# One DMA queue in another order, a table of priorities tuned again, a head by token halves, and a last tile in two half-banks, in a list-scheduled attention and GEGLU kernel

## The chip, the cores and the metric

The kernel runs on one core of one Trainium2 chip. The metric is the device time of a whole execution in microseconds (us). The kernel before takes 278.9 us as the median of three runs (278.46 to 281.0). The record marks all runs below as fast, but for the single runs (unknown) and one of the kernel before at 281.44 us (slow). A profile of a run covers the span from the first instruction to the last landing; that is 1.7 to 1.8 us less than the time of the same run.

## The reference, cut to what matters

`x` is 2048 tokens of 512 features in bf16. Path A is attention in four segments of 512 tokens with 32 heads of 16, plus a memory that is carried from segment to segment. Path B is a GEGLU of width 1792. A sigmoid gate mixes both.

```python
for s in range(4):
    logits = einsum('bhqd,bhkd->bhqk', qs, ks) * scale + mask
    a_dot  = einsum('bhqk,bhkd->bhqd', softmax(logits), vs)
    a_mem  = phi(qs) @ M / (phi(qs) @ z + 1e-6)          # memory of the segments before
    outs.append(g * a_mem + (1 - g) * a_dot)
    M = M + phi(ks)^T @ vs ; z = z + sum(phi(ks))        # phi(t) = t+1 if t > 0 else exp(t)
a = concat(outs) @ wo
b = (gelu(x @ w_gate) * (x @ w_up)) @ w_down
out = gate * a + (1 - gate) * b
```

## The kernel before

The program is a list of tasks. A list scheduler, which runs when the kernel is built, gives each task an engine and a place, using estimates of durations, priorities (`BIAS`, by kind of task) and a small model of the DMA queue. What it emits is one instruction stream per engine, with semaphore waits. All transfers go through one queue, SP's, in program order. So the order of that queue follows from the model:

```python
            cur[e] = t.finish
            avail = t.finish
            if t.nbytes:                                   # a transfer: 0.5 us (transpose 1.25) on SP, then it is on its way
                dma_free = max(t.finish + 2.2, dma_free) + t.nbytes / DMA_RATE
                avail = dma_free
```

The model lets SP issue a transfer every 0.5 or 1.25 us however much is on its way. The parts that the change touches are these (`# ...` marks cuts):

```python
    # loads, in order of rank: x0, wk, wq, wv, small vectors, wg, then
    xdma(1)                                                # x block 1, four DMA transposes
    wdma(("wu", 0), SP, ...); wdma(("wu", 1), SP, ...)
    wdma("wd", SP, ...); wdma("wo", SP, ...)
    for i in range(9):                                     # warm-up matmuls on zeros
        # ...
    for kb in range(4):                                    # x0 transposed on TensorE, 4 per feature block
        task(f"x0t{kb}", PE, [... e.transpose(XB[...], xin[:, a, ...], ident) for a in range(4)])
        # one eviction of 128x512 per block, on ACT or DVE
    # memory(s): phi(k), transposed through memory, then the outer products with v
            for t in range(4):
                dma(f"pkT{s}_{t}", SP, lambda t=t: phkt[:, :, t * 128:(t + 1) * 128], lambda t=t: kT[:, t, :],
                    [("kT", t)], [("phkt", t)], 131072, issue=1.25, transpose=True)
    # downs(s): the last tile of the last segment accumulates in one bank, one scale, one store
    # order of the tasks in the list:
    prep(0); memory(0); attention(0); xdma(2); prep(1); gates_copied(0); gates_copied(1)
    # ...
```

The softmax here doesn't subtract the row's maximum and nothing guards it: scores larger than these inputs give would overflow.

Of the kernel before, what the change touches and what calls it, by code (L numbers as in the profile page):

```python
# [13 lines left out]
ALU = mybir.AluOpType  # L14
# [13 lines left out]
DMA_RATE = 330.0e3  # L28
PATIENCE = 3.0
# [4 lines left out]
    "D0": -167, "D1": -801, "D2": 83, "D3": -2, "G0": -198, "G1": -253, "G3": -13, "GdT1": -249, "GdT2": 532,  # L34
    "GdT3": 9, "Gev1": -32, "K0": 433, "K1": 30, "K2": 94, "K3": -21, "Q0": -84, "Q1": -59, "Q2": 313, "Q3":
    -15, "U0": -1382, "U1": -543, "U2": -1, "U3": -8, "Um0": 173, "Um1": 323, "Um2": 15, "Um3": 17, "V0": 59,
    "V3": -41, "Vev0": 134, "Vev3": 374, "Vlo0": -111, "Vlo1": -31, "Vlo3": -24, "den1": 619, "den2": 394,
    "den3": 85, "denp1": 4, "denp2": 30, "denp3": 155, "exp0": -59, "exp1": -37, "exp3": 73, "exsT0": 537,
    "exsT2": 14, "exsT3": 341, "fin1": 62, "fin2": 650, "fin3": 478, "gate0": 8, "gate1": 52, "gate2": 216,
    "gate3": -16, "gelu0": -177, "gelu1": 530, "gelu2": 12, "gelu3": 107, "gexs0": 15, "gexs1": -66, "gexs2":  # L40
    278, "gexs3": 91, "gts0": -2, "gts1": -12, "gts2": -10, "gts3": -2, "kl0": 15, "kl1": 571, "kl2": 26,
    "kl3": 15, "kp0": 23, "kp1": 107, "kp2": -4, "msk0": 84, "msk1": -40, "msk2": 160, "msk3": 113, "mz0":
    402, "mz1": -18, "mz2": 72, "mzacc0": -37, "mzacc1": -9, "mzacc2": -32, "mzbd0": -100, "mzbd1": 12,
    "mzbd2": 43, "norm0": 124, "norm1": -731, "norm2": 11, "norm3": 226, "num1": 30, "num2": 47, "num3": -3,
    "nump1": 419, "nump2": -30, "oTd1": -2, "oTd2": 163, "oTd3": -179, "omg": 518, "pkT0": 8, "pkT1": 25,
    "pkT2": -8, "pkc0": -408, "pkc1": 4, "pkc2": -57, "pke0": 30, "pke1": -29, "pke2": -52, "pqc1": 40,
    "pqc2": 36, "pqe1": 118, "pqe2": 4, "pqe3": -13, "pv0": 271, "pv1": -58, "pv2": -63, "pv3": 146, "pvt0":
    -321, "pvt1": -8, "qk0": 61, "qk1": 34, "qk2": -377, "qk3": 96, "x1": -417, "x2": 6, "x3": -10
# [69 lines left out]
class Sched:  # L118
# [32 lines left out]
    def schedule(self):  # L151
# [35 lines left out]
        while len(order) < n:  # L187
# [31 lines left out]
            t.finish = st + t.est[e]  # L219
            if e == PE:  # L220
                if t.tiled == "pv" and last_pe == "pv":
                    t.finish -= PV_JOIN
                last_pe = t.tiled
            cur[e] = t.finish
            avail = t.finish
            if t.nbytes:
                dma_free = max(t.finish + 2.2, dma_free) + t.nbytes / DMA_RATE
                avail = dma_free
# [132 lines left out]
def _build(es, nc, A_x, A_wq, A_wk, A_wv, A_wo, A_beta, B_w_gate, B_w_up, B_w_down, gate_w, out):  # L361
# [94 lines left out]
    def dma(name, eng, out_ap, in_ap, reads, writes, nbytes, issue=0.5, transpose=False, bias=0.0, sm=None,  # L456
            nonc=False):
        sm = sm if sm is not None else sem("d")

        def f(e):  # L460
            if transpose:
                return e.dma_start_transpose(out_ap(), in_ap())  # L462
            if nonc:
                with nc.allow_non_contiguous_dma(reason="small vector"):
                    return e.dma_start(out_ap(), in_ap())
            return e.dma_start(out_ap(), in_ap())
        return task(name, eng, [Instr(f, reads, writes, issue, dma_sem=sm)], bias=bias, nbytes=nbytes)
# [3 lines left out]
    def wdma(key, eng, dst, src, nbytes, nonc=False):  # L471
        rank[0] -= 20.0
        dma("w_" + str(key), eng, lambda: dst, lambda: src, [], [("w", key)], nbytes, bias=rank[0], nonc=nonc)

    def xdma(s):
        for kb in range(4):
            rank[0] -= 20.0
            dma(f"x{s}_{kb}", SP, lambda kb=kb: xT[s % NX][:, kb, :],
                lambda kb=kb: A_x[0, s * 512:(s + 1) * 512, kb * 128:(kb + 1) * 128],
                [], [("xT", s % NX, kb)], 131072, issue=1.25, transpose=True, bias=rank[0] if s < 2 else 0.0)  # L480
# [30 lines left out]
    wdma(("wu", 0), SP, wu[:, :, 0:half], wur[:, :, 0:half], 917504)  # L511
    wdma(("wu", 1), SP, wu[:, :, half:DF], wur[:, :, half:DF], 917504)
    wdma("wd", SP, wd[:], r4(B_w_down), 1835008)
    wdma("wo", SP, wo[:], r4(A_wo), 524288)

    for i in range(9):
        gw = Grp(banks)
        task(f"warm{i}", PE, [Instr(lambda e, gw=gw: e.matmul(gw.f32()[:, :], warm[:, 0:128], warm, start=True,  # L518
                                                              stop=True), [wkey], [gw.key], 0.43)],
             grp=gw, bias=5000.0 - i)  # L520
    XB = XALL.bitcast(BF)
    for kb in range(4):
        task(f"x0t{kb}", PE, [Instr(lambda e, kb=kb, a=a: e.transpose(  # L523
            XB[:, kb * 1024 + a * 128:kb * 1024 + (a + 1) * 128], xin[:, a, kb * 128:(kb + 1) * 128], ident[:, :]),
            [("hT", 1, a), ("c", "ident")], [("X", kb)], mm_t(128)) for a in range(4)])
        src = XB[:, kb * 1024:kb * 1024 + 512]
        S.add(Task(f"x0ev{kb}", {
            ACT: [Instr(lambda e, kb=kb, src=src: e.activation(xT[0][:, kb, :], src, ACTF.Copy), [("X", kb)],
                        [("xT", 0, kb)], act_t(512))],
            DVE: [Instr(lambda e, kb=kb, src=src: e.tensor_copy(xT[0][:, kb, :], src), [("X", kb)],  # L530
                        [("xT", 0, kb)], dve_t(512, 2))]}))
# [56 lines left out]
    def proj_T(name, s, t, w, wkey, dst, wkeys, even=None):  # L588

        g = Grp(banks)  # L590
        xs = xT[s % NX]
        pieces(name, g, [mm(g, lambda: g.f32()[:, :], w[:, kb, t * 128:(t + 1) * 128], xs[:, kb, :],
                            [("xT", s % NX, kb), ("w", (wkey, t > 0))], kb == 0, kb == 3, 512)
                         for kb in range(4)], 2)
        if even is not None:
            task(name + "even", ACT, [Instr(lambda e: e.activation(even[0], g.f32()[:, :], ACTF.Copy,
                                                                   scale=maskc[0][:, 0:1]),
                                            [g.key, ("c", "mask", 0)], [even[1]], act_t(512, ap=True))], grp=g)
        copy_out(name + "ev", g, lambda: dst[:, t, :], lambda: g.f32()[:, :], [g.key], wkeys, 512)
# [32 lines left out]
    def prep(s):  # L632
# [21 lines left out]
        for tile in range(4):  # L654
            g = Grp(banks)
            pieces(f"V{s}_{tile}", g, [mm(g, lambda g=g: g.f32()[:, :], xT[x3][:, kb, tile * 128:(tile + 1) * 128],
                                          wv[:, kb, :], [("xT", x3, kb), ("w", "wv")], kb == 0, kb == 3, 512)
                                       for kb in range(4)], 2)
            copy_out(f"Vev{s}_{tile}", g, lambda tile=tile: Vaug[sl][:, tile, :, :, 0:16],
                     lambda g=g: g.f32()[:, :].rearrange("p (i j e) -> p j i e", j=2, e=16), [g.key],  # L660
                     [("Vaug", sl, tile)], 512)
        for j in range(2):
# [5 lines left out]
                                   [("xT", x3, kb), ("w", "gatew")], kb == 0, kb == 3, 1)  # L668
# [22 lines left out]
        if s > 0:  # L691
# [14 lines left out]
            for qt in range(4):  # L706
# [13 lines left out]
                    lambda qt=qt: otok[:, qt % 2, :], [("otok", qt % 2)], [("oT", sl, qt, t) for t in range(4)], 131072,  # L720
                    issue=1.25, transpose=True)

    def memory(s):
        sl = s % 2
        if s < NSEG - 1:
            for i in range(2):
                phi_task("pk", s, s, kT, "kT", kT, "kT", i)
            for t in range(4):
                dma(f"pkT{s}_{t}", SP, lambda t=t: phkt[:, :, t * 128:(t + 1) * 128], lambda t=t: kT[:, t, :],
                    [("kT", t)], [("phkt", t)], 131072, issue=1.25, transpose=True)  # L730
# [132 lines left out]
    def gate_mms(s, ft):  # L863
# [3 lines left out]
                                    [("xT", x3, kb), ("w", ("wg", ft // 7))], kb == 0, kb == 3, 512)  # L867
# [43 lines left out]
    def ups(s):  # L911
        sl, x3 = s % 2, s % NX
        for ft in range(NFT):
            g = Grp(banks)
            pieces(f"U{s}_{ft}", g, [mm(g, lambda g=g: g.f32()[:, :], wu[:, kb, ft * 128:(ft + 1) * 128],
                                        xT[x3][:, kb, :], [("xT", x3, kb), ("w", ("wu", ft // 7))], kb == 0,
# [5 lines left out]
    def downs(s):  # L922
# [3 lines left out]
        for tile in range(4):  # L926
            gt = 4 * s + tile
            on_x = last and tile == 3
            g = None if on_x else Grp(banks)
            key = ("X", 0) if on_x else g.key  # L930
            view = (lambda: X[0]) if on_x else (lambda g=g: g.f32()[:, :])
# [3 lines left out]
                   for fb in range(NFT)]  # L935
            seq = dwn + att if last else att + dwn
            ins = [mm(g, view, a, b, rd, i == 0, i == len(seq) - 1, 512, fkey=key)
                   for i, (a, b, rd) in enumerate(seq)]
            dep = hdep + (fins if last else [S._w[("oT", sl, tile, 3)]])
# [4 lines left out]
                    ostage[tile % N_OST][:], view(), ACTF.Copy, scale=omgt[:, gt:gt + 1]), rd, [("ost", tile % N_OST)],  # L944
                    act_t(512, ap=True))],
                DVE: [Instr(lambda e, view=view, gt=gt, tile=tile: e.tensor_scalar(  # L946
                    ostage[tile % N_OST][:], view(), omgt[:, gt:gt + 1], None, ALU.mult), rd, [("ost", tile % N_OST)],
                    dve_t(512, ap=True))]}, grp=g))
# [7 lines left out]
    sem_out = [sem("so") for _ in range(16)]  # L956
    gate_head()
# [3 lines left out]
    xdma(2)  # L961
# [29 lines left out]
    with nc.Block() as block:  # L991
# [17 lines left out]
        def _(e):  # L1009
            em.emit_stream(SP)  # L1010
            for sm in sem_out:
# [47 lines left out]
```

## Time and profile before

| | before |
|---|---|
| time, median of 3 | 278.9 us |
| span of the profiled run (its time) | 276.2 us (277.97) |
| TensorE (PE) busy | 262.9 us, 95% |
| ScalarE (ACT), VectorE (DVE), GpSimd (POOL) busy | 76%, 68%, 35% |
| PE waits for DMA, 30 to 41 us | 2.6 us |

PE is the bound. Its weight loads have a row of their own, PEld. A page of this profile is read from the top: the span, then the busy time of each engine, then the slices of a fortieth of the span each, where a low digit in PE's row is a place to look at. The waits say who ended the idle time; the timeline of SP's queue says when a transfer was issued. The lines themselves stand in the prediction. One caution, which the prediction missed: the page counts 2913 PE instructions against 2954 weight loads, so 41 matmul records are missing from this trace.

### The profile page before, as it was taken

Reading aid. Unit: us, or ns where it says so; the run is one execution under the profiler, and the core shown is the slowest. Engines: PE = TensorE matmul, PEld = TensorE weight load, DVE = VectorE, ACT = ScalarE, POOL = GpSimd, SP = SyncE. Lnnn points to the kernel's source line nnn. Section 1 sums busy time; section 2 is a strip of 40 time slices with the busy share of each in tenths; the row PEclk is TensorE's granted clock in tenths of the full one; section 3 lists DMA queues with packets and bytes.
Section 4 is the critical chain, followed back from the end, with each engine's and each line's share of the span. In section 5 each row is a group of like instructions: output and inputs, shape, how many; then the busy total and the mean of one; then the engine's idle time right before and its main releaser. Section 6 shows DMA issues by size and latency. Waiting matters only on the chain.

```text
span 276.2 us, 6911 instructions
## 1 busy us (share of the span) xinstructions
PE 262.9 (95%) x2913; PEld 121.2 (44%) x2954; DVE 187.6 (68%) x330; ACT 211.1 (76%) x178; POOL 97.5 (35%) x223
## 2 busy tenths in 40 slices
PE   8999869999999999999999999999999999989995
PEld 4444334534544444544344444444354444434442
DVE  1778738877797897797552896698752534797451
ACT  3789838999899797788978989887868777757602
POOL 8377613442101743353300762443300253352300
PEclk9999999999999999999999999999999999999999
DMA  6999960100310141123020110000020022000002
GB/s 166 290 300 357 216 125 2 23 18 2 41 40 2 38 78 38 40 42 58 20 43 0 40 33 28 21 23 19 2 44 0 19 62 56 23 0 2 0 2 76
DMA packets 31879, 16.51 MB, mean 60 GB/s; under 512 B 21352, under 2 KB 31848, under 8 KB 31848
## 3 DMA queue, kind: packets, MB, share of 16 engines
q1 hardware_dynamic: 31848, 16.07, 24.8%
q8 instruction: 23, 0.38, 0.6%
q14 instruction: 8, 0.07, 0.1%
HBM read 8.14 MB, written 2.10 MB: 37 GB/s over the span
## 4 chain that ended last, share of the span: by engine, by line
PE 85%; ACT 6%; DVE 4%; issue 2%; SPq 1%; DMA 1%; ACTq 0%; DVEq 0%
PE psW L435 68%; PE psXALL L763 8%; PE psW L812 4%; PE psW L518 1%; PE psXALL L435 1%; ACT pt L770 1%; ACT hT L897 1%; SPq L462 1%; PE psW L820 1%; ACT L897 1%; DMA phkt<-kT 1%; ACT ptl L770 1%; ACT hT L886 1%; PE psXALL L523 1%; DVE kT L610 1%
## 5 line engine op out<-in xcount | busy, mean ns | idle before, releaser
L770 ACT ACTIVATE pt<-psXALL 128x2048 bf16<-128x2048 f32 x64 | 120.0, 1875 | 31.6 <-PE psXALL L763 24.0
L774 POOL TENSOR_SCALAR_AFFINE_SELECT pt<-pt 128x256 bf16<-128x256 bf16 x128 | 57.1, 446 | 146.8 <-ACT pt L770 108.5
L435 PE MATMUL psW<-xT,wu 128*128 128x512 bf16 x215 | 51.1, 379 | 2.2 <-DVE hT L918 1.2
L435 PE MATMUL psW<-xT,wg 128*128 128x512 bf16 x218 | 50.2, 379 | 0.8 <-issue 0.5
L435 PE MATMUL psW<-wd,hT 128*128 128x512 bf16 x197 | 49.0, 379 | 1.4 <-issue 1.1
L918 DVE TENSOR_TENSOR hT<-psW,hT 128x512 bf16<-128x512 f32 x56 | 37.5, 686 | 13.7 <-PE psW L435 12.9
L827 DVE STREAM_TRANSPOSE tb<-psW 128x512 f32<-128x512 f32 x32 | 21.2, 697 | 22.9 <-PE psW L820 22.9
L435 PEld LDWEIGHTS psW<-xT,wg 128*128 128x128 bf16 x224 | 21.0, 98 | 25.3 <-issue 1.5
L435 PEld LDWEIGHTS psW<-xT,wu 128*128 128x128 bf16 x224 | 20.4, 98 | 25.9 <-DVE hT L918 1.9
L435 PEld LDWEIGHTS psW<-wd,hT 128*128 128x128 bf16 x210 | 19.0, 98 | 22.5 <-issue 2.3
L897 ACT ACTIVATE hT<-psW 128x512 bf16<-128x512 f32 x28 | 16.2, 598 | 7.0 <-PE psW L435 6.9
L774 POOL TENSOR_SCALAR_AFFINE_SELECT ptl<-ptl 128x2048 bf16<-128x2048 bf16 x8 | 17.1, 2141 | 8.7 <-ACT ptl L770 8.5
L812 PE MATMUL psW<-pt,vaug 128*17 128x192 bf16 (+3 forms) x512 | 18.8, 273 | 0.2 <-ACT hT L897 0.2
L770 ACT ACTIVATE ptl<-psXALL 128x2048 bf16<-128x2048 f32 x8 | 15.0, 1877 | 4.7 <-PE psXALL L763 4.6
L682 POOL COPY exsT<-exs 32x4 f32<-32x4 f32 x64 | 14.5, 227 | 7.6 <-ACT exs L671 3.9
L452 DVE CAST hT<-psW 128x512 bf16<-128x512 f32 x20 | 13.7, 687 | 4.8 <-PE psW L435 4.6
L435 PE MATMUL psW<-xT,wq 128*128 128x512 bf16 x59 | 15.8, 380 | 1.1 <-DMA xT<-in_A_x_dram 0.6
L435 PE MATMUL psW<-xT,wk 128*128 128x512 bf16 x63 | 15.5, 380 | 0.1
L435 PE MATMUL psW<-wo,oT 128*128 128x512 bf16 x56 | 15.1, 380 | 0.5 <-issue 0.3
L435 PE MATMUL psW<-wv,xT 128*128 128x512 bf16 x61 | 14.0, 379 | 0.4 <-ACT hT L886 0.2
L946 DVE TENSOR_SCALAR ost<-psW,omgt 128x512 bf16<-128x512 f32 x9 | 6.6, 746 | 10.8 <-PE psW L435 9.3
L812 PEld LDWEIGHTS psW<-pt,vaug 128*17 128x17 bf16 x512 | 10.3, 90 | 8.3 <-issue 3.4
(99 smaller groups left out, 305.8 us busy)
## 6 DMA issues: line engine op xcount, KB each, us to landing
out_dram<-ost SPq DMA_DIRECT2D x16, 128.0 KB, 1.7
wg<-in_B_w_gate_dram SPq DMA_DIRECT2D x2, 896.0 KB, 7.3
wd<-in_B_w_down_dram SPq DMA_DIRECT2D x1, 1792.0 KB, 11.0
wu<-in_B_w_up_dram SPq DMA_DIRECT2D x2, 896.0 KB, 11.0
vlow<-vaug SPq DMA_DIRECT2D x8, 136.0 KB, 2.8
hT<-in_A_x_dram SPq DMA_DIRECT2D x2, 256.0 KB, 2.9
wv<-in_A_wv_dram SPq DMA_DIRECT2D x1, 512.0 KB, 6.3
wo<-in_A_wo_dram SPq DMA_DIRECT2D x1, 512.0 KB, 12.0
```

The costliest lines, as they stand in the source:

```text
L435: return Instr(lambda e: e.matmul(view(), lhsT, rhs, start=first, stop=last), reads=reads, writes=[fkey if fkey is not None else g.key], e ...
L452: alts[DVE] = [Instr(lambda e: e.tensor_copy(dst(), src()), reads=reads, writes=writes, est=dve_t(n))]
L462: return e.dma_start_transpose(out_ap(), in_ap())
L682: cross = task(f"exsT{s}", POOL, [Instr(lambda e, g=g, c=c: e.tensor_copy(exsT[sl][32 * g:32 * g + 32, c:16:4], exs[32 * c:32 * c + 32, s4 ...
L763: instrs.append(Instr(lambda e, g=g, lhs=lhs, rhs=rhs, c0=c0, ncol=ncol: e.matmul(X[g][:, c0:c0 + ncol], lhs(32 * g), rhs(32 * g), start=T ...
L770: prev_exp[0] = exp_task(s, f"exp{s}_{t}{name}", [Instr(lambda e: e.activation(dst[:], XALL[:, :].rearrange("p (g c) -> p g c", g=4), ACTF ...
L774: task(f"msk{s}_{t}{name}", POOL, [Instr(lambda e, view=view, pat=pat, base=base: e.affine_select(out=view, in_=view, compare_op=ALU.is_ge ...
L812: instrs.append(Instr(lambda e, t=t, q=q, kb=kb, slot=slot, c0=c0: e.matmul(gp.f32()[32 * q:32 * q + 17, 128 * kb + 64:512], Vaug[sl][:, k ...
L827: task(f"pvt{s}_{t}_{j}", DVE, [Instr(lambda e: e.transpose(Tb[:, j, :], gp.f32()[:, :]), [gp.key], [("Tb", j)], dve_t(512))], grp=gp)
L897: lambda e, g=g, ft=ft, s=s: e.activation(hT[s % 2][:, ft, :], g.f32()[:, :], ACTF.Gelu_apprx_tanh),
L918: task(f"Um{s}_{ft}", DVE, [Instr(lambda e, g=g, ft=ft: e.tensor_tensor(hT[sl][:, ft, :], g.f32()[:, :], hT[sl][:, ft, :], ALU.mult), [g.k ...
L946: DVE: [Instr(lambda e, view=view, gt=gt, tile=tile: e.tensor_scalar(ostage[tile % N_OST][:], view(), omgt[:, gt:gt + 1], None, ALU.mult), ...
```

## The change

The intent: the transposes of phi(k) of segment 0 should not queue behind 4.2 MB of weights and a third x block (0.5 MB) that are needed later; the first projection should start as soon as the first half of x0 is there; the last output should leave sooner. The model of the queue is mended too (a transfer holds SP up once 3 us of data is waiting, transposes count double), and the table of priorities is tuned again.

```diff
+DMA_LAT = 1.6
+DMA_BACKLOG = 3.0
 BIAS = { ... }                      # all values new (cut)
+            if t.nbytes:
+                t.finish = max(t.finish, dma_free - DMA_BACKLOG)
-                dma_free = max(t.finish + 2.2, dma_free) + t.nbytes / DMA_RATE
+                dma_free = max(t.finish + DMA_LAT, dma_free) + t.nbytes / DMA_RATE
-                [], [("xT", s % NX, kb)], 131072, issue=1.25, transpose=True, ...
+                [], xk(s, kb), 262144, issue=1.25, transpose=True, ...          # also pkT, oTd: 262144
-    for i in range(9):
+    for i in range(6):
-    for kb in range(4):
-        task(f"x0t{kb}", PE, [... for a in range(4)])            # one eviction of 512
+    for u in range(2):
+        for kb in range(4):
+            gx = Grp(banks) if u else None                        # second half through the psW banks
+            task(f"x0t{kb}_{u}", PE, [... for a in range(2)], grp=gx)  # one eviction of 256
     ...
+            if on_x:                                              # the last tile: two banks of 256 columns
+                for part in (dwn, att):
+                    for u in range(2): ...                        # 14 + 14, then 4 + 4 matmuls of 256
+                # half 0 scaled on ACT, half 1 on DVE, one store of 64 KB each
     attention(0)
-    xdma(2)
+    pk0 = [t for t in S.tasks if t.name == "pkT0_3"]
+    xdma(2, after=pk0)
+    wdma(("wu", 0), SP, ..., after=pk0); wdma(("wu", 1), SP, ..., after=pk0)
+    wdma("wd", SP, ..., after=pk0); wdma("wo", SP, ..., after=pk0)
     prep(1)
```

## The prediction

> **What bounds the kernel now.** I read four views of the kernel before, in this order: the page's busy table and slices, the busy time of the engines by stretches, the waits of the tensor engine, and the timelines around the places where it stood still. The first two lines to read are the span and the tensor engine's busy time.
>
> ```profile
> span 276.2 us, 6911 instructions
> PE 262.9 (95%) x2913; PEld 121.2 (44%) x2954; DVE 187.6 (68%) x330; ACT 211.1 (76%) x178; POOL 97.5 (35%) x223
> PE   8999869999999999999999999999999999989995
> ```
>
> PE works in 262.9 of 276.2 us; ACT, the next, has 76%. So only 13.3 us of the span can be won by filling gaps, plus whatever PE work is taken out. The PE row of the slices has low digits in the first slice, around the sixth (35 to 41 us), near the end (245 us) and in the last. The stretches give their sizes (columns: stretch, its length, then busy us of each engine, clock, DMA share, GB/s).
>
> ```profile
> 1.26:30.00 28.74, 28.43 (x211) 12.94 (x214) 18.23 (x45) 21.52 (x30) 20.22 (x56) 1.00 1.01 299
> 30.00:40.00 10.00, 7.16 (x61) 2.98 (x64) 5.44 (x11) 5.68 (x6) 3.14 (x7) 1.00 1.18 145
> 40.00:245.00 205.00, 200.76 (x2380) 93.58 (x2408) 147.05 (x249) 170.11 (x135) 67.10 (x143) 1.00 0.14 29
> 245.00:250.00 5.00, 3.69 (x29) 1.42 (x25) 4.92 (x6) 2.73 (x2) 2.49 (x3) 1.00 0.00 0
> 250.00:273.20 23.20, 22.88 (x246) 10.24 (x246) 11.71 (x20) 9.90 (x7) 4.14 (x10) 1.00 0.06 18
> ```
>
> PE idle is 1.26 us before its first matmul, 0.31 to 30 us, 2.84 between 30 and 40, 4.24 over the next 205 us, 1.31 at 245, 0.32 after it, and 3.0 of output after its last matmul. The 4.24 are pieces of 0.05 and 0.16 us, mostly behind the small attention-times-value matmuls; I take them as fixed. What made the 2.84 us is in the waits of 30 to 41 us and in the timeline.
>
> ```profile
> ACT pt L770 <- PE psW L812: 3.6, 1, 3.6
> PE psW L435 <- DMA phkt<-kT: 2.0, 3, 0.9
> PE psW L435 <- DMA xT<-in_A_x_dram: 0.6, 1, 0.6
> ```
>
> PE waited three times, 2.0 us, for transposes of phi(k) of segment 0 through memory (phkt), and 0.6 us for a projection of the third x block. ACT lost 3.6 us to the same hold-up: its next exponential could not start. The issuing queue's own timeline says why those transposes came so late.
>
> ```profile
> 15.32 3.71 SPq L466 DMA_DIRECT2D wo<-in_A_wo_dram  x1
> 19.07 3.74 SPq L466 DMA_DIRECT2D wu<-in_B_w_up_dram  x2
> 22.86 9.08 SPq L462 DMA_TRANSPOSE xT<-in_A_x_dram  x4
> 32.07 0.71 SPq L466 DMA_DIRECT2D vlow<-vaug  x1
> 32.82 1.79 SPq L462 DMA_TRANSPOSE phkt<-kT  x1
> 34.66 0.59 SPq L466 DMA_DIRECT2D vlow<-vaug  x1
> 35.30 3.93 SPq L462 DMA_TRANSPOSE phkt<-kT  x3
> ```
>
> One queue issues everything in program order. The second half of phi(k) was written on DVE by 22.0 us (the add that starts at 21.34 takes 0.69), yet its transposes were issued from 32.8 to 39.2: the queue was first occupied with wo, wu and the third x block for 16.5 us. The two small copies of v (vlow) that the first attention-times-value matmuls need sat behind them too.
>
> **What the Trainium skill says.** First, "DMA: Bandwidth & Descriptors", section "Anatomy of one DMA": a semaphore wait of a DMA happens on the issuing sequencer, before dispatch. Hence an early entry blocks all later ones, and the order in the queue is a real lever; the lines above agree. Second, the same page, "Issuing engines are not separate DMA queues": all share 16 engines, so moving loads moves their traffic rather than shrinking it; 10 to 35 us runs at 294 GB/s here. Third, "TensorE: Matmul & The Clock Gate", Part 1: a cold array passes half its pulses, so a 512-column matmul costs 426.7 ns cold and 215.7 warm, and the switch comes with a free-running activity window of about 3.4 us. The trace agrees: nine warm-up matmuls take from 1.26 to 5.07 us plus a tail, weight loads start 0.427 us apart, and from 6.74 us on ten matmuls in a row take 2.33 us, or (2.33 - 0.38)/9 = 0.217 each. Fourth, its Part 4 says that transposes in the array do not count as activity in the same way; no view here shows that, but it makes cutting warm-up work a risk.
>
> **The change part by part.**
>
> (1) Six warm-up matmuls for nine: it takes out 3 x 0.427 = 1.28 us of filler. It pays only as far as x0 is there. Its two loads were issued at 0.81 and about 1.3 us and took 2.8 and 3.1 us to land, so the halves are there at about 3.6 and 4.4; the warm-up would end at 1.26 + 6 x 0.427 = 3.8. Before, the 16 transposes ran from 5.07, 0.107 us apart, and the first projection began at 6.74. Now by halves: eight transposes from about 3.9 to 4.75, eight more to 5.6, then one short eviction. ACT took 0.60 and DVE 0.43 us for 512 columns; 256 columns should be about 0.39 and 0.29. The first projection starts at about 6.0, 0.7 earlier. But the clock was seen fast only from about 6.7, so matmuls in that 0.7 us run at half speed and about 0.35 is given back; and some 0.2 more where PE waits anyway at 10.7 us for wq, whose load is not moved. I count **-0.3**, with plus or minus 1 for the clock's window.
>
> (2) The queue's order: wu, wd, wo and the third x block go behind the fourth transpose of phi(k). Those can then be issued from about 17.5 (first half of phi(k) done) to 24 us, and vlow once the last v eviction at about 18 us is done. Landing at 2.5 to 5 us, they are there by 28, before the sixth exponential. So the waits for phkt (2.0 us) go, the 0.6 us wait for the third x block goes because the retuned order need not take that projection so early, and the rest of the 2.84 shrinks with them. The moved loads cost nothing: wu is first read at 78.6 us and wd at 102.8; with 4.6 MB at the 294 GB/s seen, 16 us of traffic from about 25 us ends near 45. ACT regains its 3.6 us, so it does not become the new limit. I count **-2.6**.
>
> (3) The last output tile in half-banks: 36 matmuls of 256 columns for 18 of 512. At half of 0.217 plus about 2.5 ns fixed each, 36 x 0.111 = 4.0 against 18 x 0.217 = 3.9: +0.1. What follows the last matmul is then a 256-column DVE scale instead of an ACT one of 0.69 us. DVE took 0.75 for 512 columns, so about 0.45 for 256; the other half overlaps on ACT with PE's last matmuls. The out transfer of half the size keeps its fixed part (1.7 us to landing for 128 KB). -0.25 and +0.1 give **-0.15**.
>
> (4) The retuned priorities and transfer estimates reorder the whole list. They can remove the 1.15 us wait for a DVE multiply at 245 us (half of its 1.31 us stretch counted: -0.65), or bring one like it elsewhere. I count **-0.5**.
>
> Sum: -0.3 - 2.6 - 0.15 - 0.5 = -3.55, on 278.9: about 275.3 us. The weight of PE's real matmuls stays.
>
> **The rivals.** (a) *A new wait takes the old one's place*: phi(k) is transposed early but while wg and the first x block's successors still load (wg's second half is issued at 14.1), so transposes issue at the 2 us apiece of the x transposes rather than 1.25, and land late; or the moved loads now hold up the transposes of attention output. For it: the DMA share of 1.25 at 10 to 15 us. Against: wg's 0.9 MB is through by about 21 us, and before, phkt came even later. It would halve part 2: 276.7. (b) *The clock stays cold one window longer* because six warm-ups and transposes do not fill it: up to 3.4 us at half speed, +1.7, giving 277. For it: the skill's sentence on transposes; against: projections follow immediately. The three timed runs differ by 2.5 us (278.46 to 281.0), which could be this. (c) *Everything fits*: all 1.28 us of part 1, all 2.84 of part 2, all 1.31 at 245 us and 0.25 at the end, sum 5.7 or 273.2 us. That is just past 2%, and hard to exceed since PE remains the bound. (d) *The gap was hidden anyway*: against it stands that PE itself is the idle engine there, and the chain of waits runs through that very transfer (2.47 us of phkt).
>
> **Range and chances.** The centre is 275.3. The low end, 272.7, is rival (c) with half a microsecond of small gaps gone too; the high end, 278.2, is (a) and (b) together. A gain of over 2% means under 273.3, nearly the whole of (c): 0.12. Slower by over 2% means 284.5, which no part explains: 0.02. The rest, 0.86, is within 2%.
>
> **What would show it.** Right: phkt transposes issued before 25 us with no DMA wait of PE between 25 and 45; ACT's 3.6 us pause gone; PE busy down by about 1.3 us, its idle between first and last matmul about 6 instead of 9; first projection near 6 us; tail after the last matmul near 2.75 us. Wrong: new PE waits over 0.5 us on DVE or DMA in the reordered list, matmuls still cold past 8 us, or an ACT stall that moves to another segment.

## The result, and the profile after

The changed kernel takes 271.99 us (median of 4 runs, 271.44 to 272.78) against 279.28 for the kernel before (4 runs). The ratio is 0.9733 with a 95% interval of 0.968 to 0.9787. A ratio here is the mean time of one kernel's fast runs over that of the other's in the same rounds, so it isn't quite the ratio of the medians. The prediction was 275.3 with 272.7 as the low end, so the gain of 7.3 us was twice what was expected, and the time lies 0.7 us below the range.

The page of the changed kernel, first lines and PE's slices:

```profile
span 270.3 us, 6945 instructions
...
PE 260.6 (96%) x2928; PEld 122.1 (45%) x2969; DVE 186.9 (69%) x333; ACT 211.4 (78%) x180; POOL 96.5 (36%) x223
...
PE   7999999999999999999999999999999999999996
```

The row of nines has no dip left between the first slice and the last. The stretch of 30 to 40 us (stretch, length, busy us of PE, PEld, DVE, ACT, POOL, clock, DMA share, GB/s):

```profile
30.00:40.00 10.00, 9.79 (x129) 4.32 (x130) 8.22 (x18) 8.74 (x8) 7.62 (x27) 1.00 1.35 289
```

And all that PE waited for a transfer, from the view of waits (who waits, for whom: us in all, times, the longest):

```profile
PE psW L439 <- DMA wk<-in_A_wk_dram: 0.4, 1, 0.4
```

PE is busy for 9.79 us there instead of 7.16, and ACT for 8.74 instead of 5.68. Its only wait for a transfer is 0.4 us for wk in the head. SP's queue shows why (start, us of issue, what):

```profile
14.68 2.53 SPq L466 DMA_TRANSPOSE phkt<-kT  x2
18.53 1.35 SPq L470 DMA_DIRECT2D vlow<-vaug  x2
20.95 2.52 SPq L466 DMA_TRANSPOSE phkt<-kT  x2
23.51 1.13 SPq L470 DMA_DIRECT2D wu<-in_B_w_up_dram  x2
24.69 0.50 SPq L470 DMA_DIRECT2D wd<-in_B_w_down_dram  x1
25.23 4.88 SPq L470 DMA_DIRECT2D wo<-in_A_wo_dram  x1
30.16 9.02 SPq L466 DMA_TRANSPOSE xT<-in_A_x_dram  x4
```

The four transposes are issued from 14.7 to 23.5 us, where before they were issued from 32.8 to 39.2. The third x block still takes 9 us to issue, but PE doesn't wait for it. One thing differs from what the change intended: in the new order PE first reads the transposed phi(k) at 65.5 us (before: 36.8), so what it needs early from this queue is the two copies of v (vlow), issued at 18.5 us instead of 32.1 and 34.7. The run a_oldq below shows what happens when they are late.

### The profile page after: what moved, and what is told of

Read it like the earlier page. It is cut to its first block, busy times and chain, and to the rows that moved or that the text cites. A ratio compares the mean times of both kernels' runs of the same rounds, so it can differ in the third digit from the quotient of the medians.

```text
span 270.3 us, 6945 instructions
## 1 busy us (share of the span) xinstructions
PE 260.6 (96%) x2928; PEld 122.1 (45%) x2969; DVE 186.9 (69%) x333; ACT 211.4 (78%) x180; POOL 96.5 (36%) x223
## 4 chain that ended last, share of the span: by engine, by line
PE 89%; DVE 3%; ACT 3%; issue 2%; DMA 2%; SPq 1%; ACTq 0%
PE psW L439 72%; PE psXALL L774 8%; PE psW L823 5%; DMA wk<-in_A_wk_dram 2%; PE psXALL L439 1%; PE psW L831 1%; DVE oT L858 1%; ACT klow L638 1%; ACT pt L781 1%; ACT hT L908 1%; SPq L470 1%; DVE kpad_1 L661 0%; ACT L908 0%; DVE otok L725 0%; ACT pex L618 0%
## 5 line engine op out<-in xcount | busy, mean ns | idle before, releaser
L439 PE MATMUL psW<-wv,xT 128*128 128x512 bf16 x61 | 14.8, 380 | 0.3 <-issue 0.2
L981 DVE TENSOR_SCALAR ost<-psW,omgt 128x512 bf16<-128x512 f32 x8 | 6.0, 748 | 13.1 <-PE psW L439 13.1
L456 DVE CAST hT<-psW 128x512 bf16<-128x512 f32 x19 | 12.6, 678 | 0.9 <-PE psW L439 0.8
```

The lines of the kernel that those rows point to most:

```text
L439: return Instr(lambda e: e.matmul(view(), lhsT, rhs, start=first, stop=last), reads=reads, writes=[fkey if fkey is not None else g.key], e ...
L456: alts[DVE] = [Instr(lambda e: e.tensor_copy(dst(), src()), reads=reads, writes=writes, est=dve_t(n))]
L981: DVE: [Instr(lambda e, view=view, gt=gt, tile=tile: e.tensor_scalar(ostage[tile % N_OST][:], view(), omgt[:, gt:gt + 1], None, ALU.mult), rd,
```

## The experiments

The list scheduler makes small edits hard to test: any change of an estimate gives another order everywhere. So for most experiments the order of all instructions, with engine and PSUM bank, was written down from one of the two kernels and replayed, with only the named tasks moved. Replayed without an edit, both kernels come out with the same stream on every engine (only semaphores are named differently). Kernels that start from the kernel before have names with b_, those that start from the changed one a_. All gave correct results. Kernels in one group of runs share the runs of the kernel before, whose median was 279.0 to 279.3 us.

**Queue order alone (b_queue).** SP's queue only; the other four engines run the same streams.

```diff
   wg, second half
-  wd, wo, wu (two halves), x block 2 (four transposes)
   vlow0, phkt transpose 0, vlow1, phkt transposes 1 to 3       # segment 0
+  x block 2 (four transposes), wu (two halves), wd, wo
```

> The kernel before with one edit: the third x block and wu, wd, wo are issued after the four transposes of phi(k) of segment 0; every other engine runs the same instructions in the same order. Theory A (the prediction's step 2): the DMA waits of PE between 30 and 40 us go, 2.6 us are won, about 276.7 us. Rival B (the timed runs of before lose more to the late transposes than its profiled run shows, which was 1.3 us quicker than their median): 3.5 to 4.5 us are won, about 275, with less spread between runs. Rival C (the queue order pays only together with the retuned order of the other engines): under 1 us.

Measured: 274.39 us against 279.25; ratio 0.9839 (0.9794 to 0.9883), so 4.5 us (4.9 by the medians). Rival B of this text was right. Its span is 272.6 us. The stretch in which the kernel before lost its time:

```profile
30.00:42.00 12.00, 12.00 (x151) 5.83 (x150) 9.82 (x19) 9.63 (x9) 4.37 (x9) 1.00 0.97 311
```

PE has no idle time at all between 30 and 42 us. As PE's streams are identical, each weight load can be set against its twin: b_queue leads by 0.20 us at 10.7 us, by 3.58 us at 39.2 us, and by 3.58 us at the end. So in this pair of profiles the late transposes cost 3.4 us, all of it between 33 and 39 us, and nothing is given back later. The 2.84 us of idle time that the prediction counted there were read off wrongly in two ways. There are four stops, of 0.63, 0.49, 0.95 and 0.61 us, 2.68 in all; the other 0.16 us lie at 30.6 us, where a record is missing (next paragraph). And each stop costs 0.17 us more than its idle time: the last matmul before it is recorded as busy for 0.38 us (0.22 for the ones of 136 columns), where in a row the next one starts after 0.217 (0.065). Together that is the 3.4 us.

The 0.16 us pieces of idle time which the prediction took as fixed are not idle time either. Here is one place of the same stream, first before, then b_queue (PE's timeline, [idle before <- releaser]):

```profile
63.48 0.81 PE L435 MATMUL psW<-xT,wg 128*128 128x512 bf16 x3 [0.16 <-issue]
```

```profile
59.67 1.04 PE L502 MATMUL psW<-xT,wg 128*128 128x512 bf16 x4
```

Before shows three matmuls after a gap, b_queue shows four and no gap: the first record is missing before. In b_queue PE has all of its 2954 records, and the small gaps are gone from its trace: the 205 us in which the prediction counted 4.24 us of idle time have 0.40 there.

**The rest of the 4.5 us: the clock (b_same, b_same2 to b_same4, b_keepwarm).** The profiled run of before took 277.97 us, 1.3 less than the median of its runs. The profile of b_tail (below) came from a run at 279.25 us and had the clock at half from 38.96 to 42.37 us. Four more profiles of the unchanged kernel were taken, and one kernel with 14 matmuls on resident weights, into a bank that the next group overwrites, at the four places where PE waits:

```diff
+  3 matmuls ; Q projection, second pair (waits for x block 2)
+  4 matmuls ; phi(k)^T v, tile 0 (waits for phkt)
+  4 matmuls ; tile 1
+  3 matmuls ; tile 2
```

> The kernel before once more, for a second profile. Theory: at 278.5 us or more the granted clock is 0.5 for some 3 us after the waits at 34 to 39 us; at 278 or less it stays at 1. If a run at 279 shows no such stretch, the spread has another cause.

> Before again. Clock theory: a run at 278.8 us or more has a stretch of half clock of about 3.4 us behind the waits at 34 to 39 us, one at 278.3 or less has none. Rival (waits vary): a run at 278.8 or more with the clock at 1 throughout and longer waits before 42 us.

> As b_same2: a run at 278.8 us or more has the half-clock stretch, one at 278.3 or less has not.

> As b_same2: a run at 278.8 us or more has the half-clock stretch, one at 278.3 or less has not.

> The kernel before with 14 extra matmuls into an unused bank (results overwritten) at the four places where PE waits for the late transposes at 34 to 39 us. In a run at 279.25 us the granted clock was 0.5 from 39 to 42 us, after these waits; in the profiled run of before (277.97 us) it stayed at 1. Theory: PE's low use in the waits halves the clock afterwards in most runs of before, and costs 1.2 us at the median; with the extra matmuls the clock stays at 1 and the median falls to 278.0 to 278.5. Rival: the waits themselves vary from run to run, the clock is a side effect: 279.3 or more, since 14 matmuls are 3 us of work.

The clock records against the time of the same run, for all profiles with the old queue order and PE's unchanged middle part (b_head and b_tail differ from before only at the ends):

| profile | time, us | full clock from, us | half clock |
|---|---|---|---|
| b_head | 277.53 | 5.87 | none |
| before | 277.97 | 6.69 | none |
| b_same | 278.33 | 3.96 | none |
| b_tail | 279.25 | 4.83 | 38.96 to 42.37 |
| b_same3 | 279.44 | 5.13 | 39.27 to 42.68 |
| b_same2 | 279.55 | 6.32 | 40.45 to 43.86 |
| b_same4 | 280.15 | 6.43 | 40.57 to 43.98 |

All four runs at 279.25 us or more have a stretch of 3.41 us at half clock, right behind the waits; the three below have none. The stretches of b_same2 show it (same columns as above; the third last number is the granted clock):

```profile
38.00:40.00 2.00, 1.27 (x20) 0.71 (x24) 0.89 (x2) 0.00 (x0) 0.00 (x0) 1.00 0.62 125
40.00:42.00 2.00, 2.00 (x68) 1.50 (x62) 1.04 (x2) 1.40 (x1) 0.00 (x0) 0.61 0.04 8
42.00:44.00 2.00, 1.78 (x7) 0.74 (x7) 1.93 (x5) 0.54 (x2) 0.87 (x2) 0.53 0.00 0
```

The same stretch in the profile of before:

```profile
40.00:42.00 2.00, 1.95 (x71) 1.38 (x65) 1.29 (x3) 1.39 (x1) 0.00 (x0) 1.00 0.04 8
```

PE works in b_same2's stretch from 40 to 42 us without a gap, but at half speed for most of it. Set against the profiled run of before, weight load by weight load, the three new profiles with half clock lose 1.5 to 1.6 us in this stretch and b_tail 1.2 to 1.3. b_same, at 278.33 us, fell between the two bounds of its text and decides nothing by it; b_same2 to b_same4 came as the clock theory expected. In each of the four, the half clock begins 34.13 us after the clock had become full, which is ten times 3.41 us; in a_oldq (below) it is 30.72, nine times. "TensorE: Matmul & The Clock Gate" of the Trainium skill, Part 1, states a free-running window of 3413 ns, and this agrees. Cut into steps of 3.41 us from the moment of full clock, the emptiest step has PE busy for 1.24, 1.28, 1.73 and 1.89 us in the four profiles with half clock (the step right before it), and for 1.91, 2.08 and 2.09 in the three without. So what counts here is how much of the waiting falls into one step, and that depends on the run; 1.89 and 1.91 are too near to each other to read a threshold from them.

b_keepwarm took 278.46 us at the median of 22 runs against 279.02; ratio 0.9988 (0.9972 to 1.0004). Its profiled run, at 277.57 us, had the full clock throughout. So 3 us of extra work (14 x 0.217) cost nothing and probably won half a microsecond; by time alone the interval touches 1. The record settles it, since it lists each run's mean granted clock, and one stretch of 3.41 us at half clock in 276 us makes a mean of 0.994. All 22 runs of b_keepwarm have 0.999 or more. Of the 27 runs of the kernel before in its group, 10 have that (median 278.28 us) and 17 have 0.994 or less (279.26). In b_queue's group the kernel before has 14 (277.97) and 30 (279.54), while all four runs of b_queue and all four of the changed kernel have 0.999 or more. So the waits bring the half clock, in 47 of these 71 runs, and filling them keeps it away. At full clock before, b_queue is 3.6 us faster by the medians, near the traces' 3.4 us; the rest of its gain is the clock.

**Head alone and tail alone (b_head, b_tail).**

```diff
-  9 warm-up matmuls ; 4 x (4 transposes, eviction of 512)
+  6 warm-up matmuls ; 4 x (2 transposes, eviction of 256), twice            # b_head
-  last tile: 18 matmuls of 512, scale of 512 on ACT, store of 128 KB
+  last tile: 36 matmuls of 256, scales of 256 on ACT and DVE, two stores    # b_tail
```

> The kernel before with one edit: six warm-up matmuls for nine and x0 transposed and evicted by token halves; all the rest in the same order. Theory A (the prediction's step 1, matmuls still at half clock until 6.7 us): first projection near 6.0 us, gain 0.3 us. Rival B (the clock is fast as soon as the transposes end, as the profile after suggests): first projection near 5.7 us at 0.217 us per matmul, but waits for wk and wq take part of the 1.0 us back: gain 0.5 to 1.0 us.

> The kernel before with one edit: the last output tile in two half-banks. The prediction's step 3: gain 0.15 us; from the profile after (3.0 us after the last matmul becoming 2.66): up to 0.35 us.

Measured: b_head 279.39 us, ratio 1.0007 (0.9984 to 1.0029); b_tail 279.31 us, ratio 1.0022 (0.9996 to 1.0048). Neither brings anything that five rounds can show. b_head's first projection begins at 6.18 us instead of 6.74, but at 36.8 us, in the waits, its lead has turned into a lag of 0.57 us, and it ends with 0.4. PE's waits in b_head:

```profile
PE psW L502 <- DMA phkt<-kT: 1.4, 2, 0.8
...
PE psW L502 <- DMA xT<-in_A_x_dram: 1.0, 2, 0.8
```

So this pair of profiles doesn't show the lead lost; that a PE which is early only waits longer for the same queue is argued. The timed runs show no gain at equal clock either: 278.2 us against 277.97 for the runs at full clock. In b_tail the time after the last matmul falls from 3.02 to 2.63 us, and the half-width matmuls cost 0.05 us. That 0.39 us is less than the interval's half-width of 0.7 us.

**Queue, head and tail together (b_qht), and with shorter GpSimd masks (b_qhts).** The last stop of before is at 246 us. PE waits there for DVE to free a PSUM bank, and DVE is held up by one add. In the timeline of before around it (start, us, what):

```profile
244.54 2.12 POOL L774 TENSOR_SCALAR_AFFINE_SELECT ptl<-ptl 128x2048 bf16<-128x2048 bf16 x1 [1.61 <-ACT ptl L770]
...
244.88 2.05 DVE L847 TENSOR_TENSOR oT<-oT,ott 128x512 bf16<-128x512 bf16 x1
...
247.59 1.04 PE L435 MATMUL psW<-xT,wu 128*128 128x512 bf16 x4 [1.15 <-DVE hT L918]
```

The same add takes 0.43 us at the median of its twelve. b_qhts cuts the mask beside it:

```diff
-  affine_select(PTl viewed as 32 blocks of 64)          # 2048 columns, once
+  affine_select(PTl[:, g] viewed as 8 blocks of 64)     # 512 columns, for g in 0..3
```

> The kernel before with the queue order, the head by halves with six warm-ups and the half-bank tail, all other instructions in the old order. Head and tail brought nothing alone (ratios 1.001 and 1.002), where the head's lead of 0.4 us was lost again in the waits for the queue. If they are worth something once the queue no longer holds PE up: 0.7 to 1.3 us below the queue order alone (274.4), so 273.1 to 273.7. If they are worth nothing: 274.4.

> The same with the mask of each low block in four GpSimd instructions of 512 columns instead of one of 2048 (2.1 us). In the trace of before a 128x512 DVE add that took 0.43 us elsewhere took 2.05 us beside such a mask at 244.9 us, and PE then stood still for 1.15 us (1.5 us from weight load to weight load). Theory: the long mask holds the DVE add up; in pieces the add takes under 1 us, the stop goes and 1.0 to 1.5 us are won: 271.9 to 272.6, which is the changed kernel's time, so that the retuned table would have brought nothing but the removal of this stop. Rival: the DVE add is slow for another cause and the stop stays: as without the pieces.

Measured: b_qht 274.2 us, ratio 0.9833 (0.9807 to 0.986); b_qhts 273.1 us, ratio 0.9815 (0.9769 to 0.9861), with one of its four runs at 276.13 (mean clock 0.994) and the others at 272.6 to 273.37 (0.999 or more). So head and tail added almost nothing, and the shorter masks 1.1 us by the medians. The two intervals overlap, and it is the traces that show the latter. The same place in b_qhts:

```profile
240.89 2.90 POOL L849 TENSOR_SCALAR_AFFINE_SELECT ptl<-ptl 128x512 bf16<-128x512 bf16 x4 [1.60 <-ACT ptl L845]
...
241.23 0.59 DVE L922 TENSOR_TENSOR oT<-oT,ott 128x512 bf16<-128x512 bf16 x1
```

The add takes 0.59 us, and the stop is gone. Weight load by weight load, b_qhts leads b_qht by 0.29 us until the stop and by 1.61 us behind it, so the stop cost 1.3 us. As b_qhts differs from b_qht in the masks alone, the long mask was the cause. "SBUF — State Buffer" of the Trainium skill, section "SBUF: two separate sides", says that GpSimd and DVE share a pair of ports, that a DVE instruction with two SBUF inputs contends for it with a GpSimd one that reads SBUF, and that whoever starts first holds the pair for its whole instruction. This trace agrees: the add that started 0.34 us into the mask ended 0.27 us after it. In the changed kernel two more adds meet such a mask, 0.15 and 0.92 us after its start, and end 0.26 and 0.27 us after it (2.23 and 1.47 us long), so it is the mask's end that they wait for. b_qht also shows where the head's lead goes once the queue is mended: PE waits 0.8 us for wk and starts its q projections no earlier than b_queue does.

**The changed kernel with parts undone (a_oldq, a_oldht, a_oldbias).** a_oldq puts wd, wo, wu and the third x block back ahead of the transposes, in an otherwise unchanged order. a_oldht restores nine warm-ups, whole evictions and the single last bank. a_oldbias keeps all code of the changed kernel and takes the old table of priorities, so the scheduler makes a new order.

> The changed kernel with wd, wo, wu and the third x block issued ahead of the transposes of phi(k), as before; other engines unchanged. The projection K of segment 1 stands at 31.7 us in the changed order and overwrites what those transposes read, so PE cannot run past them. If the queue order is the larger part: 276.5 us or more (plus 4.5). If the new order hides the late transposes: under 274.

> The changed kernel with its head and tail undone: nine warm-up matmuls, x0 in whole evictions, the last tile in one bank; everything else in its order. In the old order head and tail together brought 0.2 us once the queue was right (274.4 to 274.2), since the head's lead was lost waiting for wk and wq. If the same holds here: 272.0 to 272.4. If the changed order of the first loads (wq ahead of wv and the small vectors) lets the head's lead live: 272.8 to 273.3.

> The changed kernel with the old table of priorities, so that the list scheduler makes another order under the new transfer model. If the retuned table matters little, this stays within 1 us of the changed kernel (272 to 273 us); if the table carries a good part of the gain, it falls back to 274 us or more, with new PE waits in its trace.

Measured: a_oldq 281.24 us, ratio 1.0075 (1.0046 to 1.0105), 9.2 us worse than the changed kernel and worse than before. PE's longest wait in it:

```profile
PE psW L895 <- DMA vlow<-vaug: 7.3, 1, 7.3
```

The changed order relies on the early queue: the attention-times-value matmuls stand early in PE's stream, and their small copy of v is now the thing that is stuck (its text had expected the K projection behind them to be held). The clock falls to half there from 35.24 to 42.07 us, two windows long. a_oldht: 272.79 us, ratio 0.9765 (0.9726 to 0.9804), 0.8 us by the medians; its last matmul ends 0.5 us later than in the changed kernel and its end takes 3.02 instead of 2.62 us. The intervals of both ratios overlap, so head and tail are worth about 0.8 us here by medians and traces, less surely than the rest. a_oldbias: 277.46 us, ratio 0.9943 (0.9923 to 0.9963), far from the expected 272 to 273. With the new model and the old table, stops of 0.65 us (wk), 0.71 and 1.15 us (both for DVE to free a bank, the second being that of 246 us again) and 0.29 us are there, where the changed kernel has one of 0.44. They make 2.4 of the 5.5 us; the rest wasn't taken apart. The old order with the new queue order, head and tail is at 274.2 us (b_qht), so the old table does worse under the new model than the order that it had made under the old one.

**Tries at a better kernel (a_split, a_head2).** a_split is the changed kernel with the mask in four pieces. a_head2 loads the first 128 columns of wq ahead of the rest of wk and does the first q projection while that is on its way:

```diff
   SP: x0, wk[0:128]
-  wk[128:512], wq[0:128], wq[128:512]
+  wq[0:128], wk[128:512], wq[128:512]
   PE: K tile 0
-  K tiles 1 to 3, Q tile 0
+  Q tile 0, K tiles 1 to 3
```

> The changed kernel with the low-block masks in four pieces. Its own two slow DVE adds (2.2 us) do not stop PE, so theory says no change: within 0.3 us of 272.0. If DVE's delays do reach PE somewhere: 0.5 us or more faster.

> A try at a better kernel: the changed kernel with the first 128 columns of wq loaded ahead of the rest of wk, and the first q projection moved ahead of the second k projection, so that PE has work in the 0.44 us for which it waits for wk at 6.7 us. If the wait goes and the lead lives: 271.5 to 271.8. If the wait only moves to the next load: 272.0.

Measured: a_split 272.25 us, ratio 0.9762 (0.9736 to 0.9788); a_head2 272.29 us, ratio 0.9758 (0.9729 to 0.9787). Neither beats the changed kernel. a_split confirms its text: DVE's slow adds don't reach PE in the changed order. In a_head2 the wait for wk moved to the first projection (0.37 us at 6.07 us), and the first scores are computed at 13.6 us instead of 13.3. The head is limited by what arrives, and no order tried here makes it arrive earlier. So the best version found is the changed kernel itself.

## Why the prediction was wrong

Its mechanisms were right as far as they went. Two of its terms were too small, and the larger of them lacked a cost, the half clock behind the waits.

1. **Step 2, the queue: put at 2.6 us, measured 4.5 us.** This is the step that failed. The cause and the place were as described: late transposes behind wo, wu and the third x block, PE waiting at 33 to 39 us, and the moved weights cost nothing. But the loss was read off as idle time of PE (2.84 us) in one profile. Set instruction against instruction it was 3.4 us, since each of the four stops costs more than its recorded idle time. And in most runs with the old queue, among them four of seven profiles, the waits made the clock fall to half for 3.41 us, which costs another 1.2 to 1.6 us. The page of before could not show this: its run, at 277.97 us, was one of the lucky ones, 0.9 us quicker than the median of 278.9, and the prediction did not ask why. Two slips had no effect: the moved loads are 4.7 MB and not 4.6, and the passage on semaphore waits from "Anatomy of one DMA" is not what the lines show. The entries ahead of the transposes wait for no semaphore there; their issue itself takes long (3.71 us for wo, 9.08 for the x block).
2. **Step 4, the new order: put at 0.5 us, measured at least 1.6 us.** That is b_queue against a_oldht, 274.39 to 272.79 us, which share the new queue order, the old head and the old tail; with the new head and tail it is 2.2 (b_qht to the changed kernel). The stop at 246 us was counted at half of its 1.31 us because the scheduler might bring another like it. It did not, and the stop was worth 1.3 us. A cause was at hand in the trace, one add of 2.05 us among twelve of 0.43, and was not looked for. The table that was tuned again does matter: with the old one under the new model the kernel is at 277.46 us.
3. **The 4.24 us of "fixed" small gaps** were for the most part missing records. That reading led to rival (c)'s limit of 5.7 us as "hard to exceed", and so to the low end of the range.
4. **Step 1, the head: put at 0.3 us.** Alone it brings nothing that the runs show. In the changed kernel it's about 0.5 us. Of its reasons one holds for some runs only: that matmuls are slow until 6.7 us. The clock becomes full at 3.96 to 6.92 us by the run, and in the changed kernel's profile at 5.26, before its first projection at 5.71. The other was right in kind: PE then waits for a weight, but for wk (0.44 us); wq's load was moved forward in the new order, from 4.24 to 2.88 us.
5. **Step 3, the tail: put at 0.15 us,** 0.4 us in the traces, too little for the timed runs to show. The +0.1 for narrower matmuls was not there: those of 256 columns start 0.109 us apart, half of 0.217.
6. **The rivals.** (a) did not happen: the transposes were issued from 14.7 us and 1.26 us apiece. (b) named the clock, but in the head; it was in the waits, and in the kernel before. (c), that everything fits, came nearest and was still too small. (d) was refuted by b_queue, whose lead of 3.58 us lived to the end.
7. **The signs.** Those of being right came, but PE's busy time fell by 2.3 us and not 1.3. That its idle time between the first and the last matmul is 5.8 us, where about 6 was forecast, is luck: 5.2 of it are small gaps of the kind in point 3.

The sum by experiments, each on the one before it, in medians: queue order 279.25 to 274.39; head and tail to 274.2; the stop at 246 us to 273.1; and 1.1 us to 272.0 that no single edit accounts for. That last part is left to the new order of the first loads and of the list, in which PE's waits in the head are shorter; it was not isolated. The shares depend on the sequence: undone from the changed kernel, the queue order alone is worth 9.2 us (a_oldq).

## What to carry to other kernels

When a queue issues in program order, ask of each entry not when it's needed but what stands behind it; a load that is needed 50 us later can cost 4.5 us. Don't read the price of a stop off as idle time of one profile: compare the streams instruction by instruction, look at the granted clock behind the stop and at its mean in every run, and take more than one profile where the runs differ by a per cent. And check the count of matmul records against that of weight loads before calling small gaps a fixed cost.

## What the Trainium skill lacked or had wrong

- "TensorE: Matmul & The Clock Gate", Part 1, has the clock fall after an idle window of about 3.4 us. Here it fell though no gap was over 1 us: in b_same2 the longest was 0.93 us and PE was busy for 1.89 of the 3.41 us before the fall. A window that is only partly used was enough. The same page has a case in which short idle times make the clock swing ("A second HAM failure mode"), but no share of a window that is too little.
- The same page, Part 4, says that the full clock doesn't engage for transposes in the array. Once it's there, they profit from it as others do: in b_queue the clock became full at 4.97 us and its 16 transposes, from 5.03 us on, took 1.06 us in all; in before, with the clock at half, they took 1.84.
- "DMA: Bandwidth & Descriptors" has no figure for how long an issue from SP takes when many transfers are on their way: wo took 3.71 us to issue in before and 5.64 in a_oldq, a DMA transpose of x up to 4.34 us (a_split), where a plain load takes 0.5 and a transpose 1.25 when little is on its way.
- "SBUF — State Buffer" was right on the shared ports. No page says how long a GpSimd mask holds them: an affine select took 2.12 us for 2048 columns and mostly 0.66 for 512. The price here was 1.6 us on a 0.43 us add, and 1.3 us of PE behind it.
